# Gathering each rank's rows two ranks ahead in the expert stage of an mLSTM plus mixture-of-experts kernel

## The chip, the cores and the metric

The kernel runs on one core of one Trainium2 chip. The metric is the device time of one execution in microseconds (us). Lower is better.

## What is computed

A recurrent attention (mLSTM) over 4 batches, 8 heads, 768 steps and 40 channels gives 3072 rows of 320 numbers. Each row is then sent to one of 8 experts, a two-layer network. The second part of the reference, cut to what matters here:

```python
logits = x @ w_gate                       # x: 3072 x 320
e_idx = np.argmax(logits, axis=1)         # one expert a row
gate_w = probs[np.arange(N), e_idx]       # softmax of the logits
eom = 1.0 / (1.0 + np.exp(-(x @ w_output_gate)))
for e in range(E):
    mask = e_idx == e
    h = np.maximum(x[mask] @ w1[e], 0.0)  # w1: 320 x 1024
    ye = h @ w2[e]                        # w2: 1024 x 320
    out[mask] = gate_w[mask, None] * eom[mask, e, None] * ye
```

## The kernel before

**First stage.** It computes the rows `x`, writes them with their logits to a table `xn` in HBM (3072 rows of 336 numbers), and counts and sorts the experts by how many rows they have. The sorted places are called ranks. Rank 0 is an expert chosen early: its first 256 rows are worked off inside the first stage (`pair_products`), and its remaining rows, at most 256, are rank 0 of the second stage. The other seven experts are ranks 1 to 7, with room for 512, 472, 464, 384, 368, 344 and 300 rows (`CAPS`, L32).

**Second stage.** One loop over ranks (L1366). For rank `r` it does, in program order:

- `start(r + 1)` (L1339): the expert's number is read by SP, which issues the weight loads of rank `r + 1` (`expert_load`, L569; tiles `ws`, three buffers, and `ws2`, two), and POOL issues the gather of rank `r + 1`: three small DVE operations make the row numbers `gi` (L1353, L393, L399), then one indirect DMA for each 128 rows brings them from `xn` into the tile `xg` (`expert_gather`, L589, L598; four DMAs for ranks 1 to 3, three for ranks 4 to 7). `xg` has two buffers, which ranks take in turn.
- `expert_hidden(r)` (L774): eight steps of eight matmuls into `hp` (L789); ACT makes `hh` (L790) and DVE `hl` (L791). Behind each step one piece of the weights of rank `r + 1` is split in two parts, `w1h` or `w2h` on ACT (L616, L625) and `w1l` or `w2l` on DVE (L617, L626). For rank 0 the first six steps have no piece.
- `expert_columns(r + 1)` (L759): PE transposes `xg` of the next rank (L768), 12 transposes for four blocks of rows and 9 for three; ACT and DVE copy the result to `xh` and `xl` (L769, L771). Then `scaled(r + 1)`, small DVE and ACT operations that read `xg` too (L1357, L414).
- `expert_rows(r)` (L794): per block of 128 rows 24 matmuls into `op` (L805), ACT scales them to `ob` (L808), and POOL scatters `ob` to the output (L659). Behind these stand the remaining weight pieces.
- `nc.gpsimd.drain()` on POOL (L1399).

PE, DVE, ACT and POOL run what the program lists in the order in which it is listed (`manual_schedule`), each by itself; SP issues the loads in program order as well. For `r = 0`, `start(1)` stands ahead of the loop. It gathers rank 1 with row numbers that were made in the first stage (`next`), then POOL copies rank 1's expert number to `er1`, which SP waits for, and scatters the two blocks that `pair_products` left.

Of the kernel before, what the change touches and what calls it, by code (L numbers as in the profile page):

```python
# [20 lines left out]
N, DM, E, F = B * S, H * D, 8, 1024  # L21
# [169 lines left out]
def tile_mlstm_moe(  # L191
# [18 lines left out]
    nc = tc.nc  # L210
# [67 lines left out]
    def run(gen):  # L278
        for _ in gen:
            pass  # L280
# [7 lines left out]
    def sync_after(inst, others):  # L288

        info = mybir.DependencyInfo(mybir.DependencyClass.Sync, mybir.DependencyReason.DATA)  # L290
        for o in others:
            tc.add_manual_dep(inst.ins, o.ins.name, info, reason="rows")
# [96 lines left out]
    def ids(pool, n, j0, of, name="gi"):  # L389

        yield dve(8 * n)
        pk = pool["sc"].tile([P, n, E], F32, name=name + "p")
        nc.vector.tensor_tensor(  # L393
            pk, acc[:, :, j0 : j0 + n].rearrange("p e k -> p k e"), of.unsqueeze(1).to_broadcast([P, n, E]), ALU.mult
        )
        yield dve(8 * n)
        gi = pool["sc"].tile([P, n], I32, name=name)
        with nc.allow_low_precision("exact integers"):
            nc.vector.tensor_reduce(gi, pk, AX.X, ALU.add)  # L399
        return gi  # L400
# [90 lines left out]
    er = rt.tile([P, E], I32, name="er")  # L491
    er1 = rt.tile([1, 1], I32, name="er1")
# [76 lines left out]
    def expert_load(e_reg):  # L569

        x = {}
        we = w1[bass.ds(e_reg, 1)].rearrange("a k f -> (a k) f")
        w2e = w2[bass.ds(e_reg, 1)].rearrange("a k f -> (a k) f")
        x["st1"], x["st2"] = [], []
        for kk in range(3):
            ws = wst.tile([P, F], F32, name="ws", bufs=3)
            if kk < 2:
                nc.sync.dma_start(ws, we[kk * P : (kk + 1) * P])
            else:
                nc.sync.dma_start(ws[0:64], we[256:320])  # L580
                nc.sync.dma_start(ws[64:128], we[256:320])
            x["st1"].append(ws)
        for u in range(2):
            ws = wst.tile([P, 4, DM], F32, name="ws2", bufs=2)
            nc.sync.dma_start(ws, w2e[u * 512 : (u + 1) * 512].rearrange("(c p) f -> p c f", p=P))
            x["st2"].append(ws)
        return x

    def expert_gather(pool, x, C, gi, src=xn, rows=N):  # L589

        n = (C + P - 1) // P
        x["ms"], x["C"] = [(j, min(P, C - j * P)) for j in range(n)], C
        width = src.shape[1]
        x["xg"] = xg = pool["xg"].tile([P, n, width], F32, name="xg")
        x["ids"] = gi if src is xn else xg[:, :, ID].bitcast(I32)
        for j, M in x["ms"]:
            yield "G", SCATTER
            nc.gpsimd.indirect_dma_start(  # L598
                out=xg[:, j, :] if src is xn else xg[:, j, :].bitcast(I32),
                out_offset=None,  # L600
                in_=src[:rows, :],
                in_offset=bass.IndirectOffsetOnAxis(ap=gi[:, j : j + 1], axis=0),
                bounds_check=rows - 1,
                oob_is_err=False,
            )
# [51 lines left out]
    def scatter(x, ob, j, M):  # L657

        i = nc.gpsimd.indirect_dma_start(  # L659
            out=out[:, :],  # L660
            out_offset=bass.IndirectOffsetOnAxis(ap=x["oi"][:M, j : j + 1], axis=0),
            in_=ob[:M, j, :],
            in_offset=None,
            bounds_check=N - 1,
            oob_is_err=False,
        )
        if "apart" in x:
            tc.declare_no_dep(i.ins, group="results", reason="other rows")
            tc.add_to_no_dep_group("results", i.ins)
            x["apart"].append(i)  # L670
        else:
            sync_after(i, x["before"])
# [139 lines left out]
    def row_pools(cx, pre, nb, names=("xg", "xh", "xl", "ob", "hh", "hl", "sc")):  # L812
        pool = {}
        for nm in names:
            bf = 1 if nm in ("hh", "hl") else nb
            pool[nm] = cx.enter_context(tc.tile_pool(name=pre + nm, bufs=bf, reuse_waits="tile"))
        return pool
# [14 lines left out]
    with ExitStack() as actx:  # L832
# [187 lines left out]
        with tc.manual_schedule(engines=ENG):  # L1020
# [40 lines left out]
            px, fx, apart = {}, {}, []  # L1061
# [255 lines left out]
    def flagged(bd_ps):  # L1317

        nc.vector.tensor_copy(badf, bd_ps)  # L1319
        nc.vector.tensor_copy(badi, badf)  # L1320
# [10 lines left out]
    with ExitStack() as mctx:  # L1331
        wb = mctx.enter_context(tc.tile_pool(name="wb", bufs=1, reuse_waits="tile"))
        pool = row_pools(mctx, "m", 2)
        ps1 = mctx.enter_context(tc.tile_pool(name="mps1", bufs=4, space=PSUM, reuse_waits="tile"))
        ps2 = mctx.enter_context(tc.tile_pool(name="mps2", bufs=4, space=PSUM, reuse_waits="tile"))

        lt = mctx.enter_context(tc.tile_pool(name="lt", bufs=1))
        later = lt.tile([BH, 2, S - L0], F32, name="later")
        def start(r, x):  # L1339
            x["apart"] = apart  # L1340
            if r == 1:
                run(gather(r, x, fx["next"]))
                nc.gpsimd.tensor_copy(er1, er[0:1, 1:2])
                for ob, j, M in px["leave"]:
                    scatter(px, ob, j, M)
            ev = nc.sync.value_load(er1 if r == 1 else er[0:1, r : r + 1], min_val=0, max_val=E - 1)
            x.update(expert_load(ev))
            if r > 1:
                run(gather(r, x))

        def gather(r, x, gi=None):
            if gi is None:
                nc.vector.tensor_scalar(ems[:, r], it8, erf[:, r : r + 1], None, ALU.is_equal)  # L1353
                gi = yield from ids(pool, (CAPS[r] + P - 1) // P, 0, ems[:, r])
            yield from expert_gather(pool, x, CAPS[r], gi)

        def scaled(r, x):  # L1357
            run(scale(pool, x, ems[:, r] if r else hit, nr[:, r : r + 1]))

        with tc.manual_schedule(engines=ENG):  # L1360
            x, y, parts = {**fx, "w": px["w"]}, {}, iter(())
            start(1, y)
            nc.sync.dma_start(later[:, 0], fg[:, L0:])
            nc.sync.dma_start(later[:, 1], ig[:, L0:])
            run(expert_columns(pool, (ps2, "ps2"), x))
            for r in range(E):  # L1366
                if r:
                    y = {}
                if r + 1 < E:
                    if r:  # L1370
                        start(r + 1, y)
                    pool["w"] = wa if r % 2 else wb
                    parts = chain(parts, expert_weights(dict(pool), y, 2))
                skip_parts = FIRST if r == 0 else 0
                for f, _ in enumerate(expert_hidden(pool, (ps1, "ps1"), x, (ps2, "ps2") if r == 0 else None)):
                    if r == 0 and f == 2:
                        scaled(0, x)
                    if skip_parts:
                        skip_parts -= 1
                        continue  # L1380
                    next(parts, 0)
                if r == 2:
                    bd_ps = ps2.tile([P, DM], F32, name="bd_ps", tag="ps2")[:, 0:1]
                    nc.tensor.matmul(bd_ps, flb, onesf[0:BH, 0:1], start=True, stop=True)
                    flagged(bd_ps)
                    beyond()
                if r + 1 < E:
                    run(expert_columns(pool, (ps2, "ps2"), y))
                    scaled(r + 1, y)
                else:  # L1390
                    spv = nc.values_load(spc[0:1, 0:1], engines=(mybir.EngineType.Pool,), min_val=0, max_val=128)
                for _ in expert_rows(pool, (ps2, "ps2"), x):
                    next(parts, 0)
                while y.get("parts", 10) < (6 if r == 0 else 10):
                    next(parts)
                if r == 1:
                    flb = flag(later)
                if r + 1 < E:
                    nc.gpsimd.drain()  # L1399
                x = y  # L1400
# [239 lines left out]
```

## Time and profile before

| | |
|---|---|
| median of 3 runs | 286.31 us (285.65 to 287.03) |
| the profiled execution | 287.7 us, of which the span from first to last instruction is 286.0 us |
| busy in the span | PE 266.4, DVE 176.1, ACT 144.6, POOL 83.6 us |
| TensorE clock granted, mean of the span | 0.990 |
| DMA | 46.36 MB, 162 GB/s over the span |

The second stage begins at 75.69 us of the span, with the transposes of rank 0, and PE's last matmul starts at 278.73 us. In a timeline a row gives the start, the length, the engine, the line, the operation with its output and inputs, and in brackets how long the engine had been idle and what released it. Rows of equal instructions are merged, with their count.

### The profile page before, as it was taken

To read this page: it belongs to the slowest core of one execution; us is meant where nothing else is said; L and a number is where in the kernel's file an instruction comes from. 1 tells how busy PE (TensorE), PEld (TensorE's weight loads), DVE (VectorE), ACT (ScalarE), POOL (GpSimd) and SP (SyncE) were. 2 spreads that over 40 slices of the span, in tenths; PEclk is the share of its full clock that TensorE was granted. 3 is DMA by queue.
4 is the path that set the end of the run, shared out by engine and by line. 5 is a ranking of instruction groups with operands and counts; after the bars stand their busy time and mean duration, and the time that the engine had idled before them with its cause. 6 is when DMAs were issued, how large, how long until landed. Compare 5 with 4: busy or idle time off the path is not lost. (4 is left out here: it accounts for less than half of the span.)

```text
span 286.0 us, 5637 instructions
## 1 busy us (share of the span) xinstructions
PE 266.4 (93%) x2028; PEld 246.8 (86%) x2028; DVE 176.1 (62%) x509; ACT 144.6 (51%) x335; POOL 83.6 (29%) x110
## 2 busy tenths in 40 slices
PE   7989999999899996999999999998899799899990
PEld 5868799789899785998889989998899799799980
DVE  5556899899357975648783278338718846941300
ACT  4355689894234764345652366247517526733210
POOL 5140721623260341123504250414124023212021
PEclk9999999999999999899999999999999999999998
DMA  6999999630169977073754165417544840200010
GB/s 171 327 303 303 339 354 245 229 140 26 41 186 250 335 211 257 23 211 114 254 156 138 37 219 168 139 38 231 153 141 148 236 154 20 68 25 31 1 50 9
DMA packets 22512, 46.36 MB, mean 162 GB/s; under 512 B 2877, under 2 KB 15259, under 8 KB 22476
## 3 DMA queue, kind: packets, MB, share of 16 engines
q1 hardware_dynamic: 18522, 32.78, 38.9%
q0 software_dynamic: 3632, 12.88, 13.4%
q8 instruction: 18, 0.29, 0.4%
q10 hardware_dynamic: 322, 0.25, 0.3%
q14 instruction: 18, 0.15, 0.1%
HBM read 37.84 MB, written 8.42 MB: 162 GB/s over the span
## 5 line engine op out<-in xcount | busy, mean ns | idle before, releaser
L791 DVE SCALAR_TENSOR_TENSOR hl<-hp,hh 128x256 fp32r<-128x256 f32 (+7 forms) x64 | 35.8, 561 | 56.7 <-ACT hh L790 54.0
L805 PE MATMUL op<-w2h,hh 128*128 128x320 f32 (+4 forms) x208 | 65.5, 315 | 0.8 <-DVE badf L1319 0.6
L789 PE MATMUL hp<-xh,w1h 128*128 128x256 f32 (+7 forms) x192 | 64.7, 340 | 0.6 <-ACT xh L769 0.6
L789 PE MATMUL hp<-xh,w1l 128*128 128x256 f32 (+7 forms) x192 | 64.6, 339 | 0.1
L805 PE MATMUL op<-w2h,hl 128*128 128x320 f32 (+4 forms) x208 | 64.7, 311 | 0.0
L659 POOL DMA_INDIRECT out<-ob,oi x28 | 29.6, 1056 | 120.0 <-ACT ob L808 107.8
L805 PE MATMUL op<-w2l,hh 128*128 128x320 f32 (+4 forms) x208 | 64.6, 311 | 0.0
L790 ACT ACTIVATE hh<-hp 128x256 fp32r<-128x256 f32 (+7 forms) x64 | 31.5, 495 | 35.9 <-PE hp L789 33.1
L789 PE MATMUL hp<-xl,w1h 128*128 128x256 f32 (+7 forms) x128 | 43.4, 339 | 0.1
L598 POOL DMA_INDIRECT xg<-xn,gi x24 | 29.5, 1230 | 34.5 <-DVE ki L523 7.8
L808 ACT ACTIVATE ob<-op,sc 128x320 f32<-128x320 f32 (+4 forms) x26 | 13.7, 527 | 51.0 <-PE op L805 51.0
L805 PEld LDWEIGHTS op<-w2h,hh 128*128 128x128 f32 (+4 forms) x208 | 38.1, 183 | 1.5 <-ACT xh L769 0.8
L789 PEld LDWEIGHTS hp<-xh,w1h 128*128 128x128 f32 x192 | 36.1, 188 | 3.1 <-ACT xh L769 0.9
L789 PEld LDWEIGHTS hp<-xh,w1l 128*128 128x128 f32 x192 | 36.1, 188 | 2.7 <-DVE w1l L617 0.6
L805 PEld LDWEIGHTS op<-w2l,hh 128*128 128x128 f32 (+4 forms) x208 | 38.0, 183 | 0.2
L805 PEld LDWEIGHTS op<-w2h,hl 128*128 128x128 f32 (+4 forms) x208 | 37.9, 182 | 0.2
L617 DVE TENSOR_TENSOR w1l<-ws,w1h 128x512 fp32r<-128x512 f32 x42 | 28.6, 687 | 3.3 <-ACT w1h L616 3.3
L626 DVE TENSOR_TENSOR w2l<-ws,w2h 128x640 fp32r<-128x640 f32 x28 | 22.8, 825 | 6.2 <-ACT w2h L625 5.8
L616 ACT CAST w1h<-ws 128x512 fp32r<-128x512 f32 x42 | 25.6, 611 | 1.6 <-DMA ws<-in_w 1.6
L789 PEld LDWEIGHTS hp<-xl,w1h 128*128 128x128 f32 x128 | 24.0, 188 | 1.7 <-DVE xl L771 0.3
L625 ACT CAST w2h<-ws 128x640 fp32r<-128x640 f32 x28 | 20.0, 717 | 0.0
L1188 POOL DMA_DIRECT2D xn<-xr x12 | 9.2, 763 | 31.9 <-ACT xr L1178 23.8
(222 smaller groups left out, 392.1 us busy)
## 6 DMA issues: line engine op xcount, KB each, us to landing
ws<-in_w SPq DMA_DIRECT2D x16, 640.0 KB, 4.4
ws<-in_w SPq DMA_DIRECT2D x16, 512.0 KB, 5.1
ws<-in_w SPq DMA_DIRECT2D x16, 256.0 KB, 5.2
xn<-xr POOLq DMA_DIRECT2D x12, 336.0 KB
xr<-in_on SPq DMA_DIRECT2D x3, 960.0 KB
qTt<-in_qT SPq DMA_DIRECT2D x3, 768.0 KB
qTt<-in_qT SPq DMA_DIRECT2D x3, 240.0 KB
xr<-in_on SPq DMA_DIRECT2D x1, 640.0 KB
```

Of the source, the lines that this page charges most:

```text
L598: nc.gpsimd.indirect_dma_start(out=xg[:, j, :] if src is xn else xg[:, j, :].bitcast(I32), out_offset=None, in_=src[:rows, :], in_offset=b ...
L616: nc.scalar.copy(w1h[:, kk, us], x["st1"][kk][:, us])
L617: nc.vector.tensor_tensor(w1l[:, kk, us], x["st1"][kk][:, us], w1h[:, kk, us].bitcast(F32), ALU.subtract)
L625: nc.scalar.copy(w2h[:, us], x["st2"][u][:, vs])
L626: rest.tensor_tensor(w2l[:, us], x["st2"][u][:, vs], w2h[:, us].bitcast(F32), ALU.subtract)
L659: i = nc.gpsimd.indirect_dma_start(out=out[:, :], out_offset=bass.IndirectOffsetOnAxis(ap=x["oi"][:M, j : j + 1], axis=0), in_=ob[:M, j, : ...
L789: nc.tensor.matmul(hp, a, c, start=(i == 0), stop=(i == len(mm) - 1))
L790: nc.scalar.activation(hh[:, f], hp, AF.Relu)
L791: nc.vector.scalar_tensor_tensor(hl[:, f], hp, 0.0, hh[:, f].bitcast(F32), ALU.max, ALU.subtract)
L805: nc.tensor.matmul(op[:M], a, c, start=(i == 0), stop=(i == len(mm) - 1))
L808: nc.scalar.activation(ob[:M, j], op[:M], AF.Copy, scale=x["sc"][:M, j : j + 1])
L1188: nc.gpsimd.dma_start(xn[r0 : r0 + 2 * P].rearrange("(c p) x -> p c x", p=P), rows_[b][:, c0 : c0 + 2])
```

## The change

The gathers are moved one rank forward. Rank 1's gather stays where it was. Rank 2's gather now follows `start(1)`, ahead of the loop, and in the loop `start(r + 1)` is followed by the gather of rank `r + 2`. The loads of the weights keep their place. No computation is added or left out.

```diff
         def start(r, x):
-            x["apart"] = apart
-            if r == 1:
-                run(gather(r, x, fx["next"]))
-                nc.gpsimd.tensor_copy(er1, er[0:1, 1:2])
-                for ob, j, M in px["leave"]:
-                    scatter(px, ob, j, M)
             ev = nc.sync.value_load(er1 if r == 1 else er[0:1, r : r + 1], min_val=0, max_val=E - 1)
             x.update(expert_load(ev))
-            if r > 1:
-                run(gather(r, x))
 ...
         with tc.manual_schedule(engines=ENG):
-            x, y, parts = {**fx, "w": px["w"]}, {}, iter(())
+            x, parts = {**fx, "w": px["w"]}, iter(())
+            xs = {r: {"apart": apart} for r in range(1, E)}
+            y = xs[1]
+            run(gather(1, y, fx["next"]))
+            nc.gpsimd.tensor_copy(er1, er[0:1, 1:2])
+            for ob, j, M in px["leave"]:
+                scatter(px, ob, j, M)
             start(1, y)
+            run(gather(2, xs[2]))
             nc.sync.dma_start(later[:, 0], fg[:, L0:])
             nc.sync.dma_start(later[:, 1], ig[:, L0:])
             run(expert_columns(pool, (ps2, "ps2"), x))
             for r in range(E):
-                if r:
-                    y = {}
                 if r + 1 < E:
+                    y = xs[r + 1]
                     if r:
                         start(r + 1, y)
+                        if r + 2 < E:
+                            run(gather(r + 2, xs[r + 2]))
```

POOL's queue from the gather of rank 1 on, before. `xg_1528` holds rank 1, `xg_1843` rank 2, `xg_2173` rank 3, `xg_2497` rank 4; `ob_1023` are the two blocks of the first stage, `ob_1750`, `ob_2010` and `ob_2350` those of ranks 0, 1 and 2.

```order
L598 DMA xg_1528<-xn_61,next_1455 128x336 x4
L1343 COPY er1_152<-er_151 1x1
L659 DMA out_0<-ob_1023,oi_1468 3072x320 x2
L659 DMA out_0<-ob_1750,oi_1641 3072x320 x2
L598 DMA xg_1843<-xn_61,gi_1841 128x336 x4
L659 DMA out_0<-ob_2010,oi_1748 3072x320 x4
L598 DMA xg_2173<-xn_61,gi_2171 128x336 x4
L659 DMA out_0<-ob_2350,oi_2008 3072x320 x4
```

Each gather follows the scatters of the rank two before its own. The same place in the changed program, with other buffer numbers: `xg_1573` is rank 2, `xg_1861` rank 3, `xg_2191` rank 4, and `ob_1768`, `ob_2028`, `ob_2365` are ranks 0, 1 and 2.

```order
L598 DMA xg_1528<-xn_61,next_1455 128x336 x4
L1357 COPY er1_152<-er_151 1x1
L659 DMA out_0<-ob_1023,oi_1468 3072x320 x2
L598 DMA xg_1573<-xn_61,gi_1571 128x336 x4
L659 DMA out_0<-ob_1768,oi_1659 3072x320 x2
L598 DMA xg_1861<-xn_61,gi_1859 128x336 x4
L659 DMA out_0<-ob_2028,oi_1766 3072x320 x4
L598 DMA xg_2191<-xn_61,gi_2189 128x336 x3
L659 DMA out_0<-ob_2365,oi_2026 3072x320 x4
```

Rank 2's gather now stands ahead of rank 0's scatters, and each later gather stands behind the scatters of the rank three before its own. On DVE, where the first stage ends, a piece of the difference:

```order
 L430 TENSOR_TENSOR t2_1415<-xg_982,hit_162 128x16
+L1345 TENSOR_SCALAR ems_169<-it8_92,erf_155 128x8
 L567 CAST nr_156<-ki_160 128x8
 L433 TENSOR_REDUCE z_1439<-t2_1415 128x2
...
 L393 TENSOR_TENSOR nextp_1447<-acc_149,ems_169 128x32
+L393 TENSOR_TENSOR gip_1569<-acc_149,ems_169 128x32
 L440 TENSOR_REDUCE ss_1449<-sh_1318 128x2
+L399 TENSOR_REDUCE gi_1571<-gip_1569 128x4
```

The three operations that make rank 2's row numbers now stand among the last small operations of the first stage.

## Rows read from the trace of the kernel before

**Rows 1.** The page, part 1: busy us (share) xinstructions of each engine.

```profile
PE 266.4 (93%) x2028; PEld 246.8 (86%) x2028; DVE 176.1 (62%) x509; ACT 144.6 (51%) x335; POOL 83.6 (29%) x110
```

**Rows 2.** Waits of PE from 110 us on: us in total, times, longest us.

```profile
PE xp L768 <- DMA xg<-xn,gi: 6.1, 5, 2.3
PE op L805 <- DVE badf L1319: 0.6, 1, 0.6
```

**Rows 3.** Timeline of PE: ends of the hidden stages of ranks 0 and 1.

```profile
85.54 1.47 PE L768 MATMUL xp<-ident,xg 128*128 128x128 f32 x12
86.77 0.39 PE L805 MATMUL op<-w2h,hh 128*128 128x320 f32 x1
...
88.32 0.31 PE L805 MATMUL op<-w2l,hh 128*128 128x320 f32 x1
...
109.28 0.85 PE L768 MATMUL xp<-ident,xg 128*128 128x128 f32 x3
112.48 1.56 PE L768 MATMUL xp<-ident,xg 88*128 88x88 f32 x9 [2.34 <-DMA xg<-xn,gi]
113.76 0.61 PE L805 MATMUL op<-w2h,hh 128*128 128x320 f32 x1
...
116.50 0.31 PE L805 MATMUL op<-w2l,hh 128*128 128x320 f32 x1
```

**Rows 4.** Timeline of PE: ends of the hidden stages of ranks 3 to 6.

```profile
172.87 1.15 PE L768 MATMUL xp<-ident,xg 128*128 128x128 f32 x9
173.77 0.39 PE L805 MATMUL op<-w2h,hh 128*128 128x320 f32 x1
...
199.12 0.27 PE L768 MATMUL xp<-ident,xg 128*128 128x128 f32 x1
...
201.95 0.39 PE L805 MATMUL op<-w2h,hh 128*128 128x320 f32 x1
...
223.34 0.38 PE L768 MATMUL xp<-ident,xg 128*128 128x128 f32 x2
...
225.88 0.39 PE L805 MATMUL op<-w2h,hh 128*128 128x320 f32 x1
...
246.54 0.38 PE L768 MATMUL xp<-ident,xg 128*128 128x128 f32 x2
...
248.93 0.42 PE L805 MATMUL op<-w2h,hh 128*128 128x320 f32 x1
```

**Rows 5.** Windows: PE, PEld, DVE, ACT, POOL busy (x), PEclk, DMA share, GB/s.

```profile
84.00:86.00 2.00, 2.00 (x18) 1.90 (x18) 0.91 (x3) 0.91 (x3) 0.12 (x1) 1.00 0.91 305
...
114.00:115.00 1.00, 1.00 (x6) 1.00 (x6) 0.94 (x3) 0.55 (x1) 0.00 (x0) 0.50 0.20 78
```

**Rows 6.** Timeline of POOL: gather of rank 1, two scatters, gather of rank 2.

```profile
76.47 1.01 POOL L598 DMA_INDIRECT xg<-xn,next  x1 [5.57 <-ACT ob L712]
...
83.11 1.00 POOL L659 DMA_INDIRECT out<-ob,oi  x1 [0.30 <-issue]
94.13 0.98 POOL L659 DMA_INDIRECT out<-ob,oi  x1 [10.01 <-ACT ob L808]
...
102.80 1.05 POOL L598 DMA_INDIRECT xg<-xn,gi  x1 [5.82 <-DVE w2l L626]
```

**Rows 7.** Timelines of ACT, PEld and DVE between the two stages and in rank 1.

```profile
77.12 0.76 DVE L771 TENSOR_TENSOR xl<-xp,xh 128x256 fp32r<-128x256 f32 x2 [4.46 <-ACT xh L769]
...
87.66 0.62 ACT L616 CAST w1h<-ws 128x512 fp32r<-128x512 f32 x1 [1.64 <-DMA ws<-in_w]
...
96.18 0.19 PEld L789 LDWEIGHTS hp<-xh,w1l 128*128 128x128 f32 x1 [0.56 <-DVE w1l L617]
```

**Rows 8.** DMA queue of POOL, 78 to 80 us: packets, MB, share of 16 engines.

```profile
q0 software_dynamic: 74, 0.31, 55.2%
```

**Rows 9.** DMA queues of POOL and SP from 97 to 98 us.

```profile
q1 hardware_dynamic: 73, 0.25, 70.0%
q0 software_dynamic: 30, 0.12, 31.7%
```

## Prediction

> **What bounds the kernel now.** I start with the busy times of the page: PE is busy for 93% of the span, so the kernel is bound by PE, and the question is where PE does not work [rows 1]. The list of PE's waits in the second stage has two entries: five waits of its transposes (L768) for gathered rows, 6.1 us together, the longest 2.3 us, and one of 0.6 us for a DVE copy, which this change doesn't touch [rows 2]. So the gather of the next rank comes too late at the end of some hidden stages. The timeline of PE then tells what each late gather costs, which is more than the listed idle time. Undisturbed, the end of a hidden stage takes 86.77 - 85.54 = 1.23 us from the first of 12 transposes to the first matmul of L805 [rows 3], and with 9 transposes 173.77 - 172.87 = 0.90 us [rows 4]. For rank 1 it takes 113.76 - 109.28 = 4.48 us [rows 3]; for ranks 4, 5 and 6 it takes 2.83, 2.54 and 2.39 us [rows 4]. Behind the wait of rank 1 TensorE's granted clock is at 0.50, the 1.2 GHz level [rows 5]: PE had been idle for 2.34 us, and from the eleventh matmul on it runs at full rate again.
>
> Why is the gather late? For rank 2, POOL begins it only at 102.80 us, in the middle of rank 1's hidden stage and 6.5 us before PE wants it, and it has four DMAs to issue, each over 1 us long [rows 6]. The row before it in POOL's timeline shows what it follows: the scatters of rank 0. POOL itself has time: ahead of those scatters it sits idle for 10.01 us [rows 6].
>
> **The change, part by part.** *Gathers of ranks 3 to 7.* They are issued at the same point of a rank's turn as before, behind the previous scatters, but used one rank later: instead of 6.5 us there are that plus a whole rank, some 24 us (223.34 - 199.12, [rows 4]). The buffer that gather r + 2 writes is that of rank r, whose last readers are the transposes and the scaling of rank r, one turn earlier, so the program's order holds it up nowhere. POOL issues as many DMAs as before and DVE as many small operations; they only carry the numbers of another rank. I cost this at nothing. The cover is the rank's length; if it went, the gathers would be as late as now.
>
> *Gather of rank 2.* Its three small DVE operations move from rank 1's hidden stage into the end of the first stage. DVE next sits idle for 4.46 us there, until 77.12 us, so they are hidden [rows 7]; rank 3's take their old place. Its four DMAs follow the second early scatter in POOL's queue, which ends at 83.11 + 1.00 us [rows 6]. They start near 84.4 us, and with 1.05 us each and 0.3 us between them POOL is done near 90 us, before the scatter at 94.13 us that stands behind them. They wait for no late engine: the buffer is new and the row numbers are made by then.
>
> *What goes.* The end of the hidden stage falls to its undisturbed length: rank 1 saves 4.48 - 1.23 = 3.25 us, ranks 4 to 6 save 2.83 - 0.90 = 1.93, 2.54 - 0.90 = 1.64 and 2.39 - 0.90 = 1.49 us, together 8.31 us. The clock of rank 1's first matmuls comes on top: ten of them take 116.50 - 113.76 = 2.74 us where ten take 88.32 - 86.77 = 1.55 us at full clock, so 1.19 us [rows 3]. Sum 9.50 us. What is late next in these places? The rows stage needs the last `hl` of the hidden stage only at its 24th matmul, some 3 us in, and rank 3, which has the same queues and no late gather, passes there without a wait [rows 4].
>
> *What is added.* Rank 2's gather, 4 x 128 x 336 x 4 bytes = 0.69 MB, now moves while the weights of rank 1 are being loaded, and the DMA engines are at 0.91 then, 305 GB/s [rows 5]. This counts, because ACT waits for the first of these weights until 87.66 us [rows 7]; behind that piece ACT has the last `hh` of rank 0, the copies of rank 1's columns and more weights, and the chain ends in PE waiting 0.56 us for a `w1l` at 96.18 us [rows 7]. So each microsecond that the first weights are late lengthens the whole run by about as much. No row shows these two transfers beside each other here; bounds: nothing, if the gather's first rows come after 87.66 us, as rank 1's gather, issued at 76.47 us, had 0.31 MB moved between 78 and 80 us, up to 3.5 us after its issue [rows 6, 8]; at most 0.69 MB / 0.305 MB per us = 2.3 us, if all of it goes ahead of weights that the chain needs. I take 0.5 us: the gather's first data can come 1.6 us before 87.66 us, in which it moves 1.6 x 0.155 = 0.25 MB at that queue's own rate [rows 8], and that is 0.8 us of the engines' time; the later weights have more slack, so the value lies in the lower part. A rule of the Trainium skill speaks against the change here: its page "DMA: Bandwidth & Descriptors", section "Queues, rings and completion order", says that each DMA engine takes turns between the queues that have work for it. By that rule the weights get about every second turn while the gather has any left, and the sum would carry 0.8 us rather than 0.5. The trace agrees that neither queue shuts the other out: at 97 us the two moved 0.12 and 0.25 MB within one microsecond [rows 9].
>
> *Sum.* 9.5 - 0.5 = 9.0 us less. The profiled execution took 287.7 us, so 278.7 us of its like. It lies 1.4 us above the median of the runs shown, 286.31 us; from that the forecast is **277.3 us**.
>
> **The rivals.**
>
> *The weights pay more.* The gather goes ahead of the weights whole, 2.3 us, and PE, idle at 96 us for nearly 3 us, loses the clock once more, 1.2 us. For it: a full DMA window and a chain without slack. Against it: the order of issue, since the first weights are issued near 83.5 us, ahead of the gather. Gain 9.5 - 3.5 = 6.0 us: 280.3 us. The rule on turns that I named points this way.
>
> *Another wait takes the place* at the ends of ranks 4 to 6, where DVE still has weight pieces ahead of `xl` in its queue. All of 1.93 + 1.64 + 1.49 = 5.06 us would be lost again, gain 9.0 - 5.1 = 3.9 us: 282.4 us. Against it stands rank 3 [rows 4], so I give it little.
>
> *The gathers don't come earlier*, because a wait that I misread holds them in POOL's queue until the rank before has ended. Then nothing moves: 286.3 us. Against it: POOL's idle 10.01 us at the place of the first of them [rows 6].
>
> *Slower.* POOL's DMA queue shuts out SP's while it has work. Alone it moves 0.155 MB per us [rows 8], so rank 2's gather would hold rank 1's weights for 0.69 / 0.155 = 4.5 us; if PE pays that twice, at the first `w1` pieces and again at the `w2` pieces, with the clock's 1.2 us each time, it is 11.4 us against 9.5 us: 288.2 us. It decides from a hold of 9.5 us in all. Rows 9 speak against it [rows 9].
>
> **How the numbers follow.** Forecast 0.77, weights pay more 0.15, another wait 0.03, not earlier 0.03, slower 0.02. A measurement of this kernel can tell some 0.5%, 1.4 us, from no change. The first three cases are faster by more than that: 0.95; the fourth is the same: 0.03; the last slower: 0.02. The range runs from the full 9.5 us without any contention, 276.8 us, less half the spread of the runs shown (0.7 us), to the heavy contention at 280.3 us with a little for the 1.4 us by which the profiled run stood out: 276.1 to 280.8 us. It leaves out the last three cases, 0.08, and some of the edges.
>
> **What would show it.** Right: no wait of PE on `xg` in ranks 1 to 6; 1.2 us for 12 and 0.9 us for 9 transposes up to the first matmul of L805 everywhere but at rank 2, which keeps its 0.6 us; no stretch at clock 0.50 near 110 us; rank 2's gather on POOL from about 84.4 us; ACT's wait for the first weights longer than 1.64 us by some tenths. Wrong: waits of PE for `w1l` or of ACT for `ws` of 2 us and more between 87 and 100 us, or rank 2's gather starting later than 90 us, or rows of L805 that now wait for DVE at ranks 4 to 6.

## The result, and the profile after

| | before | after |
|---|---|---|
| median of 6 runs | 286.29 us | 278.76 us |
| the profiled execution | 287.7 us | 278.76 us |
| its span | 286.0 us | 277.0 us |
| TensorE clock granted, mean of the span | 0.990 | 0.994 |

The ratio of the times is 0.974, 95% interval 0.971 to 0.977: some 7.4 us faster, against 9.0 us forecast and 278.8 against 277.3 us. The ratio leaves out one execution after that took 512.75 us and one before that took 292.09 us; the other ten lie between 277.96 and 279.41 us and between 285.40 and 287.03 us. The record doesn't name the chip of this measurement. In two later batches, on two chips, the same kernel gained only 1.3 and 1.5% (runs 5 and 9 below), and half of this document is about the difference.

The page of the changed kernel, part 1, answers to [rows 1]: PE is 2.6 us less busy. By line, the transposes (L768) are 1.6 us less and the matmuls of L805, some of which ran at half clock before, 1.2 us less.

```profile
PE 263.8 (95%) x2028; PEld 245.5 (89%) x2028; DVE 174.7 (63%) x509; ACT 143.5 (52%) x335; POOL 84.4 (30%) x110
```

PE's waits in the second stage, from 74 us on (us in total, times, longest): the entry for `xg` [rows 2] is gone, the one for `badf` stands, and one for `xl` has come. The one for `xh` lies ahead of the 110 us at which [rows 2] begin; the kernel before has it too.

```profile
PE op L805 <- DVE xl L771: 0.8, 1, 0.8
PE hp L789 <- ACT xh L769: 0.6, 1, 0.6
PE op L805 <- DVE badf L1319: 0.6, 1, 0.6
```

PE's timeline at the ends of the hidden stages of ranks 1, 2, 4 and 6, to be held against [rows 3, 4]:

```profile
109.67 1.38 PE L768 MATMUL xp<-ident,xg 128*128 128x128 f32 x12
110.84 0.39 PE L805 MATMUL op<-w2h,hh 128*128 128x320 f32 x1
...
139.09 1.42 PE L768 MATMUL xp<-ident,xg 128*128 128x128 f32 x12
141.13 0.39 PE L805 MATMUL op<-w2h,hh 128*128 128x320 f32 x1 [0.63 <-DVE badf L1319]
...
195.00 1.12 PE L768 MATMUL xp<-ident,xg 128*128 128x128 f32 x9
195.89 0.39 PE L805 MATMUL op<-w2h,hh 128*128 128x320 f32 x1
...
238.77 1.62 PE L768 MATMUL xp<-ident,xg 128*128 128x128 f32 x9
240.32 0.42 PE L805 MATMUL op<-w2h,hh 128*128 128x320 f32 x1
```

From the first transpose to the first L805 it is 1.17 us for rank 1 (4.48 before), 0.89 for rank 4 (2.83), 0.84 for rank 5 (2.54, 217.26 to 218.10), and 1.55 for rank 6 (2.39). No row there waits for a gather. Rank 6 keeps 1.55 us although nothing is late. Its nine transposes belong to rank 7, whose last block has 44 rows, and ahead of each load of that short block PE's weight loads pause for 0.17 to 0.20 us with no releaser named. The nine loads at rank 4's end, whose last block has 112 rows, take 1.03 us without a pause. PEld's timeline at rank 6's end:

```profile
239.09 0.39 PEld L768 LDWEIGHTS xp<-ident,xg 44*128 44x128 f32 x3 [0.17 <-issue]
239.64 0.33 PEld L768 LDWEIGHTS xp<-ident,xg 44*128 44x128 f32 x3 [0.17 <-issue]
240.17 0.11 PEld L768 LDWEIGHTS xp<-ident,xg 44*64 44x64 f32 x1 [0.20 <-issue]
```

The clock behind rank 1's end is at full rate (windows; the columns are those of [rows 5]):

```profile
110.00:112.00 2.00, 2.00 (x19) 2.00 (x18) 1.51 (x3) 2.00 (x5) 0.84 (x1) 1.00 0.92 339
```

What the change costs is to be looked for where rank 2's gather now lies. POOL issues it from 84.04 us, and ACT gets rank 1's first weights at 88.08 us:

```profile
84.04 1.05 POOL L598 DMA_INDIRECT xg<-xn,gi  x1 [0.30 <-issue]
85.40 1.02 POOL L598 DMA_INDIRECT xg<-xn,gi  x1 [0.30 <-issue]
86.72 1.01 POOL L598 DMA_INDIRECT xg<-xn,gi  x1 [0.30 <-issue]
88.03 1.01 POOL L598 DMA_INDIRECT xg<-xn,gi  x1 [0.30 <-issue]
```

```profile
88.08 0.62 ACT L616 CAST w1h<-ws 128x512 fp32r<-128x512 f32 x1 [3.45 <-DMA ws<-in_w]
```

That is 12.75 us after the stage's start at 75.33 us, where it was 87.66 - 75.69 = 11.97 us [rows 7]: 0.78 us later, and PE pays it at 91.07 us, where it waits 0.79 us for `xl`.

Account of the two profiles, in us: rank 1's end -3.31, the clock behind it -1.19, ranks 4, 5 and 6 -1.94, -1.70 and -0.84, the later first weights +0.78: -8.20. The first stage happened to be 0.36 shorter and the end 0.39, which makes the 9.0 us between the spans.

### The profile page after: what moved, and what is told of

Same layout as the page of the kernel before. It is cut to its first block, busy times and chain, and to the rows that moved or that the text cites. A ratio compares the mean times of both kernels' runs of the same rounds, so it can differ in the third digit from the quotient of the medians.

```text
span 277.0 us, 5637 instructions
## 1 busy us (share of the span) xinstructions
PE 263.8 (95%) x2028; PEld 245.5 (89%) x2028; DVE 174.7 (63%) x509; ACT 143.5 (52%) x335; POOL 84.4 (30%) x110
## 4 chain that ended last, share of the span: by engine, by line
PE 54%; issue 24%; DVE 8%; POOL 5%; DMA 4%; POOLq 2%; ACT 1%; SPq 0%; DVEq 0%
PE hp L789 17%; PE op L805 15%; PE hat L993 5%; POOL out L659 4%; PE two L740 3%; PE two L756 3%; PE xt_ps L1162 2%; DMA ws<-in_w 2%; POOL xg L598 2%; DMA kvt<-in_kn 2%; PE fill L1017 1%; DVE xr L1088 1%; DVE xr L1096 1%; POOLq L1399 1%; PE st L962 1%
## 5 line engine op out<-in xcount | busy, mean ns | idle before, releaser
L805 PE MATMUL op<-w2h,hh 128*128 128x320 f32 (+4 forms) x208 | 65.0, 312 | 1.4 <-DVE xl L771 0.8
L659 POOL DMA_INDIRECT out<-ob,oi x28 | 30.7, 1097 | 111.7 <-ACT ob L808 111.3
L805 PE MATMUL op<-w2h,hl 128*128 128x320 f32 (+4 forms) x208 | 64.4, 309 | 0.0
L805 PE MATMUL op<-w2l,hh 128*128 128x320 f32 (+4 forms) x208 | 64.2, 309 | 0.0
L805 PEld LDWEIGHTS op<-w2h,hh 128*128 128x128 f32 (+4 forms) x208 | 37.6, 181 | 2.1 <-DVE xl L771 1.0
L805 PEld LDWEIGHTS op<-w2h,hl 128*128 128x128 f32 (+4 forms) x208 | 37.6, 181 | 0.5 <-DVE hl L791 0.3
L805 PEld LDWEIGHTS op<-w2l,hh 128*128 128x128 f32 (+4 forms) x208 | 37.6, 181 | 0.2
```

The source lines that it names most:

```text
L659: i = nc.gpsimd.indirect_dma_start(out=out[:, :], out_offset=bass.IndirectOffsetOnAxis(ap=x["oi"][:M, j : j + 1], axis=0), in_=ob[:M, j, : ...
L805: nc.tensor.matmul(op[:M], a, c, start=(i == 0), stop=(i == len(mm) - 1))
```

## The experiments

Three theories stood at the start. One: each late gather costs its own wait, so parts of the change add up. Two: the gather of rank 2 sets off the others, and moving it alone is nearly the whole gain. Three, on the cost: rank 2's gather takes DMA time from rank 1's first weights. The runs came in three batches of four, each batch on another chip, each with the kernel before beside it. Ratios are to that kernel in the same batch, with a 95% interval. In the second and third batch the kernel before itself spread from 284.31 to 291.44 us and from 284.96 to 292.56 us, so the ratios there are less sure than their intervals say: against the six quickest of its seventeen executions (median 286.8 us) run 5 gains only 0.7%, against the ten quickest (287.4 us) run 9 gains 0.9%. Kernels of one batch are better compared by their own medians.

**Run 1: only rank 2's gather early.** The later gathers stay one rank ahead.

```diff
                     if r:
                         start(r + 1, y)
-                        if r + 2 < E:
-                            run(gather(r + 2, xs[r + 2]))
+                        if r > 1:
+                            run(gather(r + 1, y))
```

> Only rank 2's rows are gathered early; ranks 3 to 7 stay one rank ahead. Theory (every late gather costs its own wait, and rank 2's early transfer costs the weights of rank 1): the end of rank 1's hidden stage falls from 4.5 to 1.2 us and its clock stays up (-3.3 - 1.2 us), the pause near 90 us stays (+0.8 us), ranks 4 to 6 keep their late gathers. 3.7 us less than the kernel before. Rival (the first late gather sets the rest of the run off its beat, and the later waits follow from it): the later waits shrink too, and the whole 7.5 us are won here.

Measured: 282.94 us beside 287.05, ratio 0.986 (0.981 to 0.991). The profiled execution was the longest of the six, 285.5 us, so it is read for its waits and not for its time. PE's list has the late gathers of ranks 5 to 7 left, at the ends of ranks 4 to 6:

```profile
PE xp L768 <- DMA xg<-xn,gi: 4.0, 4, 2.0
```

**Run 2: all but rank 2's gather early.** Rank 2's gather goes back into the loop, behind `start(2, ...)`, with rank 3's behind it.

```diff
-            run(gather(2, xs[2]))
 ...
                         start(r + 1, y)
+                        if r == 1:
+                            run(gather(2, y))
                         if r + 2 < E:
                             run(gather(r + 2, xs[r + 2]))
```

> Ranks 3 to 7 are gathered two ranks ahead, rank 2 at its old place, with rank 3 right behind it. Theory: rank 1's end keeps its 4.5 us and the low clock, and ACT waits only 1.6 us for the first weights; ranks 4, 5 and 6 end in 0.9, 0.85 and 1.55 us. 1.9 + 1.7 + 0.8 = 4.4 us less than before, and together with the kernel with rank 2 alone the whole change. Rival (the first late gather sets off the others): under 1 us.

Measured: 282.31 us, ratio 0.986 (0.980 to 0.991). Ranks 4 to 6 end as in the changed kernel (0.89, 0.84, 1.55 us), and rank 1's end waits as it did before, in PE's timeline and in the window behind it:

```profile
111.72 0.33 PE L768 MATMUL xp<-ident,xg 128*128 128x128 f32 x1 [2.37 <-DMA xg<-xn,gi]
112.31 1.11 PE L768 MATMUL xp<-ident,xg 88*128 88x88 f32 x9 [0.27 <-DMA xg<-xn,gi]
113.21 0.39 PE L805 MATMUL op<-w2h,hh 128*128 128x320 f32 x1
```

```profile
113.00:114.00 1.00, 1.00 (x10) 1.00 (x8) 0.77 (x2) 1.00 (x3) 0.69 (x2) 1.00 0.90 356
```

What follows from both: 4.1 us and 4.7 us, 8.8 us together. The changed kernel itself was not in this batch, but runs 3 and 4, which differ from it only in rank 2's gather, gain 8.4 and 9.3 us. So each late gather costs its own wait, and theory two falls. And one thing that neither theory had: PE was idle for 2.37 us and the clock stayed at 1.00, while after 2.34 us in the profile of before it was at 0.50 [rows 3, 5].

**Run 3: rank 2's gather later.** Its row numbers are made where they were, its DMAs follow rank 0's first scatter, away from the first weights.

```diff
-            run(gather(2, xs[2]))
+            second = gather(2, xs[2])
+            for _ in range(3):
+                next(second)
 ...
-                for _ in expert_rows(pool, (ps2, "ps2"), x):
+                for k, _ in enumerate(expert_rows(pool, (ps2, "ps2"), x)):
+                    if r == 0 and k == 1:
+                        run(second)
                     next(parts, 0)
```

> As the change, but the DMAs of rank 2's gather stand behind the first scatter of rank 0 on POOL, some 10 us later, past the loading of rank 1's weights. Theory (the weights pay for the early transfer): ACT's wait for the first weights falls back from 3.4 to about 1.6 us, PE's pause near 90 us from 0.8 to 0.4 us or less, and rank 1's end stays at 1.2 us: 0.8 us below the change, 8.2 us below before. Rival (that pause has another cause, such as SP issuing the loads at another time): within 0.2 us of the change.

Measured: 278.63 us, ratio 0.972 (0.968 to 0.976), no wait for `xg`. ACT waits 2.7 us for the first weights; the expected fall to 1.6 us did not come.

**Run 4: more rows beside the weights.** Three more gathers (0.52 MB), read by nothing, follow rank 2's.

```diff
             run(gather(2, xs[2]))
+            again = lt.tile([P, 3, ID], F32, name="again")
+            for j in range(3):
+                nc.gpsimd.indirect_dma_start(out=again[:, j, :], in_=xn[:N, :], ...)
```

> As the change, with 0.52 MB more gathered right behind rank 2's gather, three DMAs of the same rows into a tile that nobody reads. Theory (contention on the DMA engines, in turns): the first weights are already mostly there when these rows move, so the first pause stays near 0.8 us and the later pieces of rank 1's weights, which had slack, use it up: 0 to 1 us over the change. If POOL's queue shut out SP's: 0.52 / 0.155 = 3.4 us over the change. If contention plays no part: within 0.2 us of the change.

Measured: 277.74 us, ratio 0.970 (0.965 to 0.975). On this chip more traffic costs nothing, and less of it (run 3) gains nothing that can be told apart. ACT's wait was 2.52 us here, and 2.55 us in run 2, where no gather is near:

```profile
87.24 0.62 ACT L616 CAST w1h<-ws 128x512 fp32r<-128x512 f32 x1 [2.52 <-DMA ws<-in_w]
```

ACT's wait also depends on when ACT is ready for the weights, so the path of PE is the better measure. From the stage's start to the first transpose at rank 1's end PE takes 33.77 us in run 1 and 33.36 us in run 4, with the gather beside the weights, and 33.47 us in run 2 and 33.55 us in run 3, without; it was 33.59 us before, and 34.34 us in the profile after. So the 0.78 us in the account above isn't shown to come from the gather.

**Runs 5 to 8, on a second chip. Run 5: the changed kernel again.**

> The changed kernel itself, again on the chip, so that the three kernels beside it are compared with it in one batch. In its first measurement it was 7.4 us under the kernel before (ratio 0.974). Theory: all of its gain is the late rows, whose single parts added up to 8.2 us in the runs with one part alone, so it comes out 7 to 8.5 us under the kernel before. Rival (the contention of rank 2's gather costs a few tenths to 0.8 us in some executions): the same number, and ACT's first wait for ws differs by 1 us and more from the first measurement's 3.45 us while the total stays within 0.5 us of it.

Measured: 284.82 us, ratio 0.987 (0.982 to 0.992), not the 0.974 of before. The ends of ranks 1 to 6 are as short as they were (1.18, 2.05, 0.90, 0.88, 0.85, 1.56 us), so the whole loss lies ahead of them: from the first transpose of the stage to the first L805 of rank 0 it takes 92.20 - 75.53 = 16.67 us instead of 86.23 - 75.33 = 10.90. Timelines of ACT and PE in that stretch:

```profile
82.16 0.21 ACT L435 ACTIVATE z<-z 128x2 f32<-128x2 f32 x1
85.57 0.38 ACT L790 ACTIVATE hh<-hp 128x256 fp32r<-128x256 f32 x1 [3.21 <-PE hp L789]
90.74 0.94 ACT L790 ACTIVATE hh<-hp 128x256 fp32r<-128x256 f32 x3 [4.79 <-PE xp L768]
```

```profile
86.47 0.39 PE L789 MATMUL hp<-xh,w1h 128*128 128x256 f32 x1 [2.03 <-issue]
88.50 0.37 PE L768 MATMUL xp<-ident,xg 128*128 128x128 f32 x1 [0.32 <-issue]
...
90.68 1.87 PE L768 MATMUL xp<-ident,xg 128*128 128x128 f32 x8 [0.35 <-issue]
```

In the first measurement ACT went from `z` to `hh` without a pause:

```profile
81.92 0.20 ACT L435 ACTIVATE z<-z 128x2 f32<-128x2 f32 x1
82.03 0.71 ACT L790 ACTIVATE hh<-hp 128x256 fp32r<-128x256 f32 x2
```

Here ACT stands for 3.21 and 4.79 us, and the releasers named can't be what it waited for: the eight matmuls of the `hp` it needs are long done, since PE runs on to 84.4 us. The standstill begins ahead of the gather: ACT could have gone on at 82.4 us, and the gather's first DMA is issued at 84.27 us. PE then stops too; in run 9's profile its wait there is named, 3.53 us for DVE's `hl`, which follows ACT's `hh`. SP's loads, which followed each other within 0.3 us, start at 87.76, 89.16 and 90.64 us:

```profile
83.38 2.15 SPq L578 DMA_DIRECT2D ws<-in_w  x2
87.76 0.02 SPq L580 DMA_DIRECT2D ws<-in_w  x1
89.16 0.01 SPq L581 DMA_DIRECT2D ws<-in_w  x1
```

The clock goes with it, to the 1.2 GHz level:

```profile
88.00:90.00 2.00, 0.96 (x4) 0.39 (x3) 0.00 (x0) 0.00 (x0) 1.00 (x1) 0.50 1.07 349
...
92.00:94.00 2.00, 2.00 (x10) 1.97 (x9) 1.98 (x5) 2.00 (x6) 0.00 (x0) 0.50 0.97 240
```

POOL alone goes on, one DMA every 1.3 us, the last of the gather's until 89.27 us; 1.5 us after that ACT is at work again. The loading of code doesn't explain it as far as the profile shows: the queues of kind "instruction" bring one packet each after 80.0 and 83.0 us here, after 79.75 and 82.75 us in the first profile after, and none between 84 and 92 us in either.

**Run 6: the kernel before without POOL's drain.** Why is a gather late at all when POOL is free? In the kernel before, rank 2's row numbers are ready 5 us before POOL begins at 102.80 us [rows 6]; DVE's timeline:

```profile
97.26 0.19 DVE L399 TENSOR_REDUCE gi<-gip 128x4 int32<-128x32 f32 x1
```

This run keeps the gathers in their old places.

```diff
-                if r + 1 < E:
-                    nc.gpsimd.drain()
```

> The kernel before with its gathers where they were, but without the drain that stands on POOL between the scatters of a rank and the next gather. Theory A (the drain holds the gather: in the kernel before, rank 2's gather begins at 102.80 us although its row numbers are made by 97.5 us and POOL is free at 97.0 us; the others begin 2.8 to 3.9 us behind the last scatter): rank 2's gather begins near 97.5 us, 5 us earlier, and the later ones some 2.5 us earlier; the rows of rank 2 come in time, those of ranks 4 to 6 are late by under 0.5 us where they were late by 0.9 to 1.6 us. The time falls by 6 to 8 us, nearly all that the change brought, with no gather moved to another rank's turn. Theory B (the gather waits for its row numbers or for DVE, or the queue itself takes that long behind a scatter): gathers begin where they did, PE's five waits for xg of 6.1 us stay, the time stays within 1 us of the kernel before.

Measured: 285.32 us, ratio 0.989 (0.985 to 0.994). POOL's timeline and PE's wait for `xg`:

```profile
95.49 1.40 POOL L659 DMA_INDIRECT out<-ob,oi  x1 [0.48 <-DMA ws<-in_w]
98.16 1.52 POOL L598 DMA_INDIRECT xg<-xn,gi  x1 [1.27 <-issue]
```

```profile
PE xp L768 <- DMA xg<-xn,gi: 0.3, 1, 0.3
```

The gather begins 1.27 us after the last scatter instead of 5.82 [rows 6], rank 3's 1.33 instead of 2.98 us, and 0.3 us is left of 6.1 us of waits. Theory A holds for the gathers: PE reaches rank 6's first L805 at 240.34 us, as the changed kernel does in its first profile (240.32). But the time did not fall by 6 to 8 us. POOL's last scatter, first of the changed kernel and then of this one, is at the same place:

```profile
271.29 0.94 POOL L659 DMA_INDIRECT out<-ob,oi  x1 [2.55 <-ACT ob L808]
```

```profile
271.31 0.94 POOL L659 DMA_INDIRECT out<-ob,oi  x1 [2.55 <-ACT ob L808]
```

The spans end at 277.0 and 282.1 us. Without drains there are 9.8 us behind the last scatter instead of 4.8. That the kernel's end now waits for what the drains waited for is likely, but no row names it.

**Run 7: the flag's matmul behind rank 2's rows.** On the changed kernel; it concerns PE's wait for `badf`.

```diff
-                if r == 2:
-                    bd_ps = ps2.tile([P, DM], F32, name="bd_ps", tag="ps2")[:, 0:1]
-                    ...
                 if r + 1 < E:
                     run(expert_columns(pool, (ps2, "ps2"), y))
 ...
                 while y.get("parts", 10) < (6 if r == 0 else 10):
                     next(parts)
+                if r == 2:
+                    bd_ps = ps2.tile([P, DM], F32, name="bd_ps", tag="ps2")[:, 0:1]
+                    ...
```

> The changed kernel with the one matmul into bd_ps and the small DVE operations behind it moved from rank 2's end of the hidden stage to the end of its rows. Theory: PE's wait there (0.6 us for badf) is the one that is left on the path between ranks, so the end of rank 2's hidden stage falls from 2.04 us to 1.2 us and the time by 0.6 to 0.8 us against the changed kernel. Rival: the PSUM buffer was only one of two things that were late there, and xl of the columns takes its place: the wait is named otherwise, the time stays within 0.3 us.

Measured: 284.1 us, ratio 0.985 (0.980 to 0.990), 0.7 us under run 5, which the intervals don't separate. The profile shows the step itself: rank 2's end takes 1.16 us instead of 2.05.

```profile
144.25 1.36 PE L768 MATMUL xp<-ident,xg 128*128 128x128 f32 x12
145.41 0.39 PE L805 MATMUL op<-w2h,hh 128*128 128x320 f32 x1
```

**Run 8: run 7 without the drain.** The edit is that of run 6.

> As the run before it, and without the drain on POOL too. Theory: once gathers are issued two ranks ahead, the drain is off the path: its removal moves the later gathers 2.5 to 8 us earlier on POOL and changes the time by no more than 0.4 us against the run with the drain. Rival: gathers that start earlier meet the weights of the next rank in the DMA queues, ACT's waits for ws grow and the time rises by 0.5 us or more; or DVE's small operations were held through POOL, and it falls by as much.

Measured: 289.63 us, ratio 1.011 (1.007 to 1.016), 5.5 us over run 7. Neither theory had the reason, which is that of run 6: rank 6's first L805 is at 245.38 us against 245.10, the last scatter ends at 277.29 against 277.01, and the span goes on for 10.0 us instead of 5.3. With gathers two ranks ahead the drain is off the path between ranks, and leaving it out makes the end 4.7 us longer.

**Runs 9 to 12, on a third chip. Run 9: the changed kernel once more.** The question is now the standstill of run 5.

> The changed kernel itself, on whichever chip this batch gets, as the base for the three beside it. In its first profile SP issued rank 1's first weights at 82.51 us, 1.53 us before rank 2's gather began on POOL, and no engine stood still; in the second one SP issued them at 83.38 us, 0.89 us before, and between 84 and 91 us PE, ACT and SP stood still together for over 5 us with nothing named that they waited for. Theory T (the lead decides: the stall comes when the gather begins before SP has got out more than the first two loads): a lead of 1.5 us goes with some 278 to 279 us, one of 0.9 us with 284 to 285 us. Rival C (the chip decides, whatever the lead): either time can come with either lead.

Measured: 284.7 us, ratio 0.985 (0.980 to 0.990). The lead was 84.53 - 83.70 = 0.83 us, and ACT stands for 4.73 and 3.57 us. Both theories allow it.

**Run 10: weights later.** `er1` is copied behind the first early scatter.

```diff
             run(gather(1, y, fx["next"]))
-            nc.gpsimd.tensor_copy(er1, er[0:1, 1:2])
-            for ob, j, M in px["leave"]:
+            for k, (ob, j, M) in enumerate(px["leave"]):
                 scatter(px, ob, j, M)
+                if k == 0:
+                    nc.gpsimd.tensor_copy(er1, er[0:1, 1:2])
```

> The changed kernel with the copy of rank 1's expert number moved on POOL behind the first of the two early scatters, so that SP issues rank 1's weights 1.3 us later and rank 2's gather begins ahead of them or with them. Theory T: PE, ACT and SP stand still between 84 and 92 us for 5 us and more, on any chip; the time is 284 us or more, 5 us over the undisturbed changed kernel. Rival C, on a chip where the changed kernel runs undisturbed: only the 1.3 us of the later loads, and no row of PE with an idle time of 2 us and no releaser.

Measured: 284.89 us, ratio 0.986 (0.980 to 0.992). SP's first load comes at 85.48 us, 1.8 us later than in run 9, and nothing gets worse: ACT stands for 3.42 and 4.87 us.

**Run 11: weights earlier.** `er1` is copied ahead of the last two DMAs of rank 1's gather.

```diff
-            run(gather(1, y, fx["next"]))
+            first = gather(1, y, fx["next"])
+            for _ in range(3):
+                next(first)
             nc.gpsimd.tensor_copy(er1, er[0:1, 1:2])
+            run(first)
```

> The changed kernel with the copy of rank 1's expert number moved ahead of the last two of the four DMAs of rank 1's gather, so that SP issues rank 1's weights 2.6 us earlier and has all six loads out before rank 2's gather begins. Theory T: no standstill between 84 and 92 us on any chip; where the changed kernel stands still this run is 5 us and more faster than it, where it doesn't the two are within 1 us, with a lower wait of ACT for ws. Rival C: where the changed kernel stands still this one does too, at 284 us and more. A third way: the standstill follows the loads and comes now beside rank 1's gather or the scatters, between 79 and 84 us.

Measured: 286.38 us, ratio 0.998 (0.994 to 1.001). The lead is now 3.7 us and the standstill is there all the same, so theory T falls. ACT's timeline:

```profile
82.96 0.20 ACT L435 ACTIVATE z<-z 128x2 f32<-128x2 f32 x1
88.89 0.38 ACT L790 ACTIVATE hh<-hp 128x256 fp32r<-128x256 f32 x1 [5.73 <-remote]
91.09 0.66 ACT L790 ACTIVATE hh<-hp 128x256 fp32r<-128x256 f32 x2 [1.81 <-remote]
```

It is even 1.7 us slower than run 9. Its profiled execution was the fastest of twelve, 284.40 us, and doesn't show why.

**Run 12: rank 2's gather later, and the flag's matmul behind the rows.** The edits of runs 3 and 7 together.

> Rank 2's gather behind rank 0's first scatter, as in the run with that edit, and the matmul into bd_ps with its small DVE operations behind rank 2's rows. Theory: nothing of the gather lies beside the first loads of rank 1's weights, so there is no standstill on any chip, and PE's wait of 0.6 us at rank 2 is gone (its end falls from 2.04 to 1.2 us): 276.5 to 278 us, under both kernels, whatever the changed kernel gives in this batch. Rival: the standstill does not come from that gather, and this run shows it wherever the changed kernel does.

Measured: 278.64 us, ratio 0.963 (0.957 to 0.968), 6.1 us under the changed kernel on the same chip, and the best ratio of all. The stage begins at 77.27 us in this profile, and yet:

```profile
83.89 0.20 ACT L435 ACTIVATE z<-z 128x2 f32<-128x2 f32 x1
86.69 1.21 ACT L790 ACTIVATE hh<-hp 128x256 fp32r<-128x256 f32 x4 [2.59 <-PE hp L789]
```

ACT stands once, for 2.59 us, the clock stays at 1.00, and rank 2's end is at 1.16 us. From the stage's start to the first transpose at rank 1's end PE takes 34.28 us, where run 9 took 40.33. That is the gather's place; the flag accounts for 0.9 us, by rank 2's end. (The first stage was 1.46 us longer in this profile, so the spans differ by less than the sum.)

**What the standstill is, as far as the runs go.** The sum of ACT's two pauses behind `z` is, on the second and third chip, 8.0 us (run 5), 8.1 (7), 8.2 (8), 8.3 (9), 8.3 (10) and 7.5 (11), all with rank 2's gather at that place, and 2.2 us (run 6) and 2.6 us (12) without it. The profile of before has 1.06 + 1.13 = 2.2 us as well; it did not hold PE up there:

```profile
83.58 0.38 ACT L790 ACTIVATE hh<-hp 128x256 fp32r<-128x256 f32 x1 [1.06 <-PE hp L789]
85.09 0.94 ACT L790 ACTIVATE hh<-hp 128x256 fp32r<-128x256 f32 x3 [1.13 <-PE hp L789]
```

The difference is some 5.7 us, and the gather's four DMAs keep POOL issuing for 5.0 us (84.27 to 89.27 in run 5). Each time ACT is back at work 1 to 1.8 us after POOL's last DMA of the row. That the gather's place sets off the long standstill is shown by run 12 beside run 9, since run 7 shows that the flag does not cure it. How it does so is not shown. The timing suggests that on these chips ACT and SP hardly get on until POOL has issued what it has there, but POOL's issuing alone is not enough: in run 5 it issues the four DMAs of rank 1's gather from 76.32 to 81.27 us, and ACT's pauses behind its first `hh` are 0.50 and 0.56 us in that time. Nor does SP stop altogether: in run 11 it issues three of its loads between 84.49 and 88.85 us.

On the chip of runs 1 to 4 the pauses are two of 0.56 us, each the normal wait for `hp`, with the gather at that place (runs 1 and 4) and without it (2 and 3), and so they are in the first profile after. The profile of before thus looks like run 6's, on the second chip, and not like those of the first batch. Whether the two profiles of the first measurement come from one chip is not on record, and each chip was seen in one batch only, so that it is the chip which decides is not shown either. What ACT and SP wait for no row names. A run of the kernel before with other DMAs of POOL at this place was not tried.

## Why the prediction was right, and where it wasn't

- *What bounds, and why the gathers are late.* Right that they follow the scatters. What holds them is more than the order: for most of the delay it is the drain between the two (run 6), a line that the prediction did not weigh. Moving the gathers or taking out the drain removes the same waits.
- *Rank 1's end, 3.25 us:* 3.31. *Ranks 4 and 5, 1.93 and 1.64 us:* 1.94 and 1.70. *Rank 6, 1.49 us:* 0.84. This term was mis-sized: the undisturbed length of nine transposes was taken from rank 3 [rows 4], and rank 7's 44-row block makes it 1.55 us.
- *The clock, 1.19 us:* gone in the profile of after, as said. But run 2 has the same wait without the loss, so it is no fixed price; that the gain came in full here is in part luck.
- *The step to the median.* The profiled execution after took 278.76 us, where 278.7 "of its like" was forecast; the median is the same 278.76, not 277.3. The prediction counted the clock's 1.19 us as gain and took off 1.4 us besides, because the profiled execution of before lay that much above its median. If that excess was mostly the clock, which run 2 makes possible but does not show, it was taken twice: 286.31 - (9.0 - 1.2) = 278.5 us.
- *The cost beside the weights, 0.5 us, bounds 0 and 2.3.* In the first measurement's pair of profiles 0.78 us, and in runs 1 to 4 nothing that can be told apart. On the other two chips 5.7 us (PE's path in run 5 beside run 6) and 6.1 us (run 9 beside run 12), outside the bounds, and with it the time, 284.8 and 284.7 us, is outside the range. The bounds came from bytes over bandwidth; the price there is a standstill of ACT, SP and PE, about as long as POOL issues the gather. So this step failed on two chips of those seen, and that the first measurement came out near the forecast was luck as far as this term goes.
- *The rule on turns.* The Trainium skill, page "DMA: Bandwidth & Descriptors", section "Queues, rings and completion order", has each DMA engine take turns between queues. The rows agree that both queues move: between 88 and 90 us of the profile after, SP's queue moved 0.35 MB and POOL's 0.17. The 0.8 us worked out from it can't be shown: run 4 moves 0.52 MB more and is no slower.
- *The rivals.* No other wait took the place at ranks 4 to 6, and the gathers did come earlier. "The weights pay more" named the right place and the second loss of the clock, and on the second and third chip the time lost is even larger than its 3.5 us, but neither it nor the slower rival had the mechanism: no queue is shut out, and issuing the loads earlier (run 11) doesn't help.
- *The signs.* No wait for `xg`, 1.2 and 0.9 us at the ends but for rank 6, no 0.50 near 110 us, the gather on POOL from 84.04 us (84.4 said), ACT's wait above 1.64 us: 3.45, by more than the tenths expected. Of these 1.81 us only 0.78 are later weights; for the other 1.03 us ACT was ready earlier, since the `hh` ahead of that wait ended 9.31 us after the stage's start instead of 10.34.

## What to carry to other kernels

When a transfer comes late, look not only at what stands ahead of it in its queue but at what its engine waits for between the two; here taking out one drain removed nearly the same waits as the reordering, and made the end of the kernel 5 us longer. Place an early gather where nothing starts up: behind rank 0's first scatter it does the same for rank 2, without lying in the row of POOL's DMAs at which ACT and SP stood. And where one profiled execution stands above its median, ask whether its excess is one of the terms that the change removes before subtracting it again.

## What was not expected of the hardware

- On two chips ACT paused for 7.5 to 8.3 us in all, and SP and PE with it, while POOL issued the gather's indirect DMAs behind two scatters (2.2 to 2.6 us without the gather), with no releaser that explains it; on the chip of runs 1 to 4 it was 1.1 us in all.
- A drain on POOL after two scatters held the next indirect DMA until 5.82 us after the last of them; without it, 1.27 us. Without drains 9.8 us stood behind the last scatter instead of 4.8, and 10.0 instead of 5.3 in another pair.
- TensorE's clock fell to 0.50 after an idle time of 2.34 us in one execution and stayed at 1.00 after 2.37 us, with 0.27 us more right behind it, in another.
- Nine transposes whose last block has 44 rows took 1.62 us where nine with a last block of 112 rows took 1.12 us.
